# Two bank pairs in rotation, one reduce for the row maximum, a written-out order, and a rounding copy that reads SBUF

## The chip, the cores and the metric

The kernel runs on one core of a Trainium2 chip. The metric is the device time of one execution in microseconds (us): the median of three executions, before the change 281.76 us. Five engines work side by side, each through its own queue in the order in which the instructions were written: TensorE (PE, with its weight loads shown apart as PEld), VectorE (DVE), ScalarE (ACT), GpSimd (POOL), and SyncE (SP), which issues transfers. They wait for each other through semaphores.

## What is computed

A sliding-window attention with sink tokens, and behind it a gated block with a short causal convolution. The shapes are 4 batches, 8 heads, 768 positions, head width 64; the block is 512 wide.

```python
def _attn_ref(q, k, v, n_sink, window):          # n_sink = 4, window = 128
    scores = scale * np.matmul(q, k.transpose(0, 1, 3, 2))
    ...
    keep = is_sink | in_window
    scores = np.where(keep, scores, -1000000000.0)
    scores = scores - np.max(scores, axis=-1, keepdims=True)
    a = np.exp(scores)
    a = a / (np.sum(a, axis=-1, keepdims=True) + 1e-09)
    return np.matmul(a, v).astype(np.float32)

def _moe_ref(x, w_val, conv_w, w_out):           # x: attention output, heads side by side
    ...
    for k in range(K):                           # K = 5 taps
        gate_pre += conv_w[k][None, None, :] * xp[:, k:k + S, :]
    gate = 1.0 / (1.0 + np.exp(-gate_pre))
    val = x @ w_val
    return (gate * val @ w_out).astype(np.float32)
```

The three parameters of the block arrive as 64-bit floats and are decoded on the chip into a rounded high part and a rest, each in single precision.

## The kernel before

The work is cut into 24 steps. A step is one batch, one third p of the positions (256 of them) and one half of the heads (four heads, as two groups g = 0 and 1). Two steps with the same batch and third make a block m of the gated part, so there are 12 blocks. A query sees its window and the four sink keys, so the scores of one step and one group are two banks of PSUM wide.

One step runs through these events, named as in the tables below:

- kq, vv: loads of keys and queries, and of values (SP; three buffers each).
- s0, s1 (`scores`, L364): the scores of one group, 16 matmuls with 64 rows and 32 columns of the array, into the one tile `ss` of two PSUM banks. Then DVE copies the window's edge over by a mask (L369) and, in four fused instructions, adds the mask, scales by -1/8 and takes the minimum, which is minus the maximum (L374). Their output `sx` lies in SBUF, so `ss` is free as soon as DVE is done.
- e0, e1 (`exps`, L382): ACT takes the exponential of `sx`, four instructions each with a sum. rec (L387, L388) is one over the sum on DVE, norm (L396 to L403) the product on POOL, once for the window and once for the sinks.
- tx, ty (`probs_t`, L413): four transposes each on PE, into two single banks `tr`. px (L435, L437, DVE) and py (L444, ACT) write them to `wt`, with the triangle masks. sk (L418) and ts transpose the sinks' part.
- vl, si (`values`, L461, and `sinks`, L468): the attention output, into the tile `xv` of two banks. There is only one `xv`, and it is free when the convolution has read it.
- xc (L478) copies `xv` to SBUF as `xt`; xh (`x_high`, L482) rounds `xv` to the short form that the fast matmuls take; xl (L492, POOL) is the rest. hd (L486) puts the last four columns of the previous third ahead of `xv`. c4 (L496, POOL) and c0, c1 (`conv`, L504, DVE, eight instructions) are the five taps, th (L509) the gate.

A block adds v0 to v3 (`val`, L523, twelve matmuls each; v0 and v1 fill one bank, v2 and v3 the other), g0, h0, l0 and g1, h1, l1 (L534 on DVE, L538 on ACT, L542 on POOL: gate times value, its rounded form, its rest), o0 to o3 (`outp`, L553, six matmuls each) and t0, t1 (`store`).

The PSUM banks: two for `ss`, two for `xv`, two for `tr` and two for `acc`, which takes v, o, sk, the decoding of the weights and the fillers in turn.

wv and wo with a letter are the weights' loads (l) and the six stages of their decoding (a to f), for four pieces each. A filler (`busy`, L225) multiplies zeros, only to keep PE at work; there are 46 in all besides the two at L218.

The order of everything is a table of numbers: each event has a time in units of steps (`WHEN`, `EARLY`, `DECODE`, L36 to L91), the events are sorted by it (L596), and each engine gets its instructions in that order. The scheduler moves nothing.

Of the kernel before, what the change touches and what calls it, by code (L numbers as in the profile page):

```python
# [8 lines left out]
F32 = mybir.dt.float32  # L9
# [26 lines left out]
WHEN = dict(kq=-1.9615, vv=-0.3611, s0=-0.1928, e0=0.4814, s1=0.3255, e1=0.5848, rec=0.6245, vl=1.4302, norm=0.667,  # L36
            tx=0.9562, ty=1.2383, sk=1.1919, ev=1.1901, yv=1.3942, ts=1.226, val=1.8427, si=1.874, xc=2.044,
            xh=2.2668, hd=2.0069, xl=2.2917, c4=2.0938, c0=2.2838, c1=2.5363, th=2.774, v0=0.4208, v1=0.4433,
            v2=0.7542, g0=0.6699, v3=0.8679, h0=0.7252, l0=1.0416, g1=0.9504, h1=1.0551, l1=1.282, o0=1.3729,
            o1=1.5265, o2=1.3969, t0=2.127, o3=2.081, t1=2.5321, cw=-67.148)  # L40

EARLY = {("kq", 0): -111.3041, ("vv", 0): -51.6322, ("s0", 0): -67.4875, ("e0", 0): -63.9472, ("s1", 0): -63.8218,
# [39 lines left out]
DECODE = {("wv", "l"): (-149.6305, -105.8601, -107.8005, -68.4578),  # L82
# [9 lines left out]
FIRST = 16  # L92

FILL = {("scores", (0, 0)): 6, ("decode_weights", ("wv", 0, 4)): 5, ("scores", (1, 0)): 7, ("scores", (2, 1)): 4,
        ("scores", (3, 0)): 10}
SKA = 6

# [708 lines left out]
```

## Time and profile before

| | us |
|---|---|
| runs | 282.0, 281.76, 279.97 |
| median | 281.76 |
| span of the profiled execution, first to last instruction | 279.6 |
| last matmul begins / last store's copy begins | 273.24 / 273.67 |

The profiled execution is close to the fastest run: its span is 0.4 us under it. Busy times add up the stretches in which an engine had an instruction under way, so two instructions that overlap count once. The end of a matmul is modelled, so of matmuls in a row the distance from start to start is what one costs. The granted clock is 1.00 when PE runs at its full rate.

### The profile page before, as it was taken

Reading aid. Unit: us, or ns where it says so; the run is one execution under the profiler, and the core shown is the slowest. Engines: PE = TensorE matmul, PEld = TensorE weight load, DVE = VectorE, ACT = ScalarE, POOL = GpSimd, SP = SyncE. Lnnn points to the kernel's source line nnn. Section 1 sums busy time; section 2 is a strip of 40 time slices with the busy share of each in tenths; the row PEclk is TensorE's granted clock in tenths of the full one; section 3 lists DMA queues with packets and bytes.
Section 4 is the critical chain, followed back from the end, with each engine's and each line's share of the span. In section 5 each row is a group of like instructions: output and inputs, shape, how many; then the busy total and the mean of one; then the engine's idle time right before and its main releaser. Section 6 shows DMA issues by size and latency. Waiting matters only on the chain.

```text
span 279.6 us, 9649 instructions
## 1 busy us (share of the span) xinstructions
PE 264.6 (95%) x3748; PEld 211.1 (75%) x3752; DVE 221.2 (79%) x827; ACT 181.0 (65%) x605; POOL 175.4 (63%) x226
## 2 busy tenths in 40 slices
PE   8897599999999999999999999999999999999991
PEld 3444358769878879789789788788788788798880
DVE  5899969997879787986977987996896898887510
ACT  3799949838757765764875784685676667564421
POOL 3378956883965874675585757648658729647330
PEclk9999989999999999999999999999999999999997
DMA  6993952028416515516417317326336241020202
GB/s 191 328 373 129 303 158 96 4 85 291 140 49 212 157 38 194 155 41 211 140 40 246 101 67 225 101 84 205 97 93 212 87 134 56 6 75 0 77 5 82
DMA packets 27396, 36.95 MB, mean 132 GB/s; under 512 B 2256, under 2 KB 23760, under 8 KB 27344
## 3 DMA queue, kind: packets, MB, share of 16 engines
q1 hardware_dynamic: 27344, 36.27, 40.4%
q8 instruction: 31, 0.51, 0.8%
q14 instruction: 21, 0.17, 0.2%
HBM read 29.97 MB, written 6.29 MB: 130 GB/s over the span
## 4 chain that ended last, share of the span: by engine, by line
PE 77%; POOL 7%; DVE 7%; ACT 5%; issue 1%; POOLq 0%; ACTq 0%
PE acc L523 23%; PE acc L553 21%; PE xv L461 11%; PE ss L364 9%; PE tr L413 5%; PE acc L225 3%; PE xv L468 3%; POOL wx L396 2%; DVE sg L504 2%; ACT w L382 2%; DVE sx L374 2%; POOL sg L496 1%; ACT xt L478 1%; POOL xl L492 1%; POOL wol L179 1%
## 5 line engine op out<-in xcount | busy, mean ns | idle before, releaser
L396 POOL TENSOR_TENSOR wx<-w,sm 128x512 f32<-128x512 f32 x48 | 49.2, 1047 | 59.9 <-DVE sm L388 53.2
L504 DVE SCALAR_TENSOR_TENSOR sg<-xv,cw,sg 128x256 f32<-128x256 f32 x192 | 78.9, 475 | 5.9 <-POOL sg L496 5.9
L382 ACT ACTIVATE w<-sx,ngm 128x132 f32<-128x132 f32 x192 | 75.1, 399 | 4.1 <-DVE ngm L374 4.1
L523 PE MATMUL acc<-xh,wvh 128*128 128x256 f32 x192 | 49.3, 291 | 0.4 <-ACT xh L482 0.4
L523 PE MATMUL acc<-xh,wvl 128*128 128x256 f32 x192 | 47.1, 279 | 0.0
L374 DVE CUSTOM_DVE_ANT_0 sx<-ss,mask 128x132 f32<-128x132 f32 x192 | 45.2, 292 | 1.6
L553 PE MATMUL acc<-woh,gh 128*128 128x512 f32 x96 | 40.0, 416 | 0.0
L364 PE MATMUL ss<-k,q 64*32 64x168 f32 x1536 | 38.5, 309 | 1.4 <-DVE ngm L374 0.8
L523 PEld LDWEIGHTS acc<-xh,wvh 128*128 128x128 f32 x192 | 36.1, 188 | 3.8 <-DVE sg L504 1.3
L553 PE MATMUL acc<-wol,gh 128*128 128x512 f32 x96 | 38.1, 397 | 0.3 <-POOL wol L179 0.3
L553 PE MATMUL acc<-woh,gl 128*128 128x512 f32 x96 | 38.1, 396 | 0.0
L382 ACT ACTIVATION_READ_ACCUMULATOR w<-sx,ngm 128x1 f32 x192 | 37.2, 194 | 0.0
L461 PEld LDWEIGHTS xv<-wt,v 64*64 64x64 f32 x1024 | 30.3, 133 | 8.1 <-issue 5.1
L523 PEld LDWEIGHTS acc<-xh,wvl 128*128 128x128 f32 x192 | 36.1, 188 | 0.0
L542 POOL TENSOR_TENSOR gl<-sg,gh 128x512 fp32r<-128x512 f32 x24 | 31.5, 1312 | 5.7 <-ACT gh L538 5.7
L461 PE MATMUL xv<-wt,v 64*64 64x192 f32 (+2 forms) x1024 | 34.5, 278 | 0.5 <-ACT wt L444 0.5
L496 POOL TENSOR_TENSOR sg<-xt,cw 128x512 f32<-128x512 f32 x24 | 25.2, 1051 | 11.4 <-ACT xt L478 11.3
L364 PEld LDWEIGHTS ss<-k,q 64*32 64x32 f32 x1536 | 22.4, 106 | 12.8 <-issue 3.6
L492 POOL TENSOR_TENSOR xl<-xt,xh 128x512 fp32r<-128x512 f32 x24 | 30.9, 1289 | 1.7 <-ACT xh L482 1.7
L523 PE MATMUL acc<-xl,wvh 128*128 128x256 f32 x192 | 30.9, 281 | 0.9 <-POOL xl L492 0.9
L413 PE MATMUL tr<-ident,wx 128*128 128x128 f32 x192 | 28.2, 274 | 0.0
L523 PEld LDWEIGHTS acc<-xl,wvh 128*128 128x128 f32 x192 | 26.0, 188 | 1.4 <-POOL xl L492 1.3
(110 smaller groups left out, 423.5 us busy)
## 6 DMA issues: line engine op xcount, KB each, us to landing
k<-in_kt_dram SPq DMA_DIRECT2D x23, 408.0 KB, 4.0
v<-in_vt_dram SPq DMA_DIRECT2D x16, 384.0 KB, 3.3
out_dram<-osb SPq DMA_DIRECT2D x24, 256.0 KB, 2.1
q<-in_qt_dram SPq DMA_DIRECT2D x23, 256.0 KB, 4.3
raw<-in_w_val_dram SPq DMA_DIRECT2D x4, 512.0 KB, 6.7
v<-in_vt_dram SPq DMA_DIRECT2D x8, 256.0 KB, 4.2
raw<-in_w_out_dram SPq DMA_DIRECT2D x4, 512.0 KB, 6.2
vs<-in_vsk_dram SPq DMA_DIRECT2D x8, 128.0 KB, 4.1
```

The lines of the kernel that those rows point to most:

```text
L364: nc.tensor.matmul(ss[e * QB:(e + 1) * QB, j, c * n + x0:c * n + x1], q[js, g, (4 * c + e) * QB:(4 * c + e + 1) * QB], k[js, g, (2 * c + e ...
L374: nc.vector.tensor_tensor_reduce(out=sx[:, j, c], in0=sv[:, j, c, :PK], in1=mask[:, c if p == 0 else 2], op0=ALU.add, op1=ALU.min, scale=- ...
L382: nc.scalar.activation(out=w[:, g, j, c], in_=sx[:, j, c], func=AF.Exp, scale=-1.0, bias=ngm[:, g, j, c:c + 1], accum_out=sm[:, g, j, c:c ...
L396: nc.gpsimd.tensor_tensor(out=t[:, n].rearrange("p c h x -> p h c x"), in0=w[:, :, :, at], in1=sm.to_broadcast([P, 4, 2, D]), op=ALU.mult)
L413: nc.tensor.transpose(out=x[:, o:o + P], identity=ident, in_=ws[s][:, n, c, 2 * g:2 * g + 2].rearrange("p j x -> p (j x)"))
L461: nc.tensor.matmul(acc[o * D:(o + 1) * D, g, x0 + h * D:x0 + (h + a1 - a0 + 1) * D], v[js, g, n], t[js, g, n, a0:a1 + 1].rearrange("p a r ...
L492: nc.gpsimd.tensor_tensor(out=xl[:, g], in0=xts[s], in1=xh[:, g].bitcast(F32), op=ALU.subtract)
L496: nc.gpsimd.tensor_tensor(out=sg[s // 2][:, g], in0=xts[s], op=ALU.mult, in1=cw[:, g, KT - 1:].to_broadcast([P, 2, PQ]))
L504: nc.vector.scalar_tensor_tensor(out=g, in0=x, scalar=a, in1=g, op0=ALU.mult, op1=ALU.add)
L523: nc.tensor.matmul(acc[:, h], a[:, kc, cs], x[:, kc], start=(n == 0), stop=(n == 11))
L542: nc.gpsimd.tensor_tensor(out=gl, in0=g, in1=gh.bitcast(F32), op=ALU.subtract)
L553: nc.tensor.matmul(acc, a[:, kc, ts], x[:, kc], start=(kc + n == 0), stop=(kc + n == 5))
```

## The change

Eight banks are given out anew. Two pairs of banks rotate: each scores half, and each step's transposes (now tx alone, eight in a row), take the next pair. `xv` keeps its two banks. The two single banks are now called homes: a user takes the first from a list and puts it back where its reader is issued. For the first two blocks the values are copied out of their bank by ACT (`val_copy`, y0 and y1), so that the gate's product reads SBUF.

For the second and third p the maximum is one `tensor_reduce` over the two banks and a small product with -1/8, and the exponentials read the pair in PSUM. The first p keeps the four fused instructions. The mask has two planes instead of three.

The rounding copy xh reads `xt` in SBUF instead of `xv` in PSUM.

The tables of numbers are gone. The order is a list of names. The identity, the two sign matrices, the blanks and the warm-up of the exponential are events of that list too, the index patterns of the masks are issued in one go, and three of the first loads (q of step 0 in two parts, wv piece 0) are issued from ACT's queue. Fillers: 38, and six at the start. The keys of steps 6 and 10 are loaded ahead of those of step 5, into the same three buffers.

```diff
-WHEN = dict(kq=-1.9615, vv=-0.3611, s0=-0.1928, e0=0.4814, s1=0.3255, e1=0.5848, rec=0.6245, vl=1.4302, norm=0.667,
...
+ORDER = """
+fill.7 load_conv wvl.0 fill.10 masks kq.0 conv_weights wvl.2 wva.0 wvb.0 wvc.0 wvd.0 s0.0 s1.0 e0.0 blanks
+fill.5 signs wva.2 wvb.2 e1.0 rec.0 wve.0 wvl.1 wva.1 wvb.1 fill.4 kq.1 s1.1 wvc.2 wvf.0 wvd.2 kq.2 wol.1 s0.1
...
+COPIES = 2
...
-    ps_t = ctx.enter_context(tc.tile_pool(name="ps_t", bufs=2, space=PSUM))
-    ps_a = ctx.enter_context(tc.tile_pool(name="ps_a", bufs=2, space=PSUM))
...
+    pairs = [ps_s.tile([P, 2, 512], F32, name=f"pr{n}") for n in range(2)]
...
+    def pair():
+        pairs.append(pairs.pop(0))
+        return pairs[-1]
...
+    homes = [ps_a.tile([P, 512], F32, name=f"ac{n}") for n in range(2)]
...
     def busy(n):
-        t = ps_a.tile([P, 512], F32, name="acc", tag="acc")
+        t = homes.pop(0)
...
+        homes.append(t)
...
+            (nc.scalar if s == 0 else nc.sync).dma_start(out=q[:, hs], in_=qt[b, gs, :, p * PQ:(p + 1) * PQ].rearrange("g p x -> p g x"))
...
+        ss = pair()
...
+        if p:
+            sxs[s, g] = sv
+            nc.vector.tensor_reduce(out=ngm[:, g], in_=sv[:, :, :, :PK], axis=mybir.AxisListType.X, op=ALU.max)
+            nc.vector.tensor_scalar(out=ngm[:, g], in0=ngm[:, g], scalar1=-0.125, scalar2=None, op0=ALU.mult)
+            return
...
-                nc.scalar.activation(out=w[:, g, j, c], in_=sx[:, j, c], func=AF.Exp, scale=-1.0,
+                nc.scalar.activation(out=w[:, g, j, c], in_=sx[:, j, c, :PK], func=AF.Exp,
+                                     scale=0.125 if steps[s][1] else -1.0,
...
-    def probs_t(s, n):
-        trs[s, n] = x = ps_t.tile([P, 512], F32, name="tr", tag="tr")
...
+    def probs_t(s):
+        trs[s] = x = pair()
+        for n in range(2):
...
     def x_high(s):
-        g, o = slice(2 * steps[s][2], 2 * steps[s][2] + 2), KT - 1
-        nc.scalar.activation(out=xs[s // 2][0][:, g], in_=accs[s][:, :, o:o + PQ], func=AF.Copy)
+        nc.scalar.activation(out=half(xhs, s, "xh", F32R), in_=xts[s], func=AF.Copy)
...
+    def val_copy(m, u):
+        t = p2.tile([P, 4, P, 2], I32, name="vc", tag="raw", bufs=4)
+        x = t.rearrange("p k m t -> p (k m t)")[:, :2 * PQ].bitcast(F32)
+        nc.scalar.activation(out=x, in_=vacc[m, u], func=AF.Copy)
+        homes.append(vacc[m, u])
+        vacc[m, u] = x
...
-        for _, f, args in sorted(events, key=lambda e: e[0]):
+        for n in ORDER.split():
+            f, args = events[n]
             f(*args)
-            if (f.__name__, args) in FILL:
-                busy(FILL[f.__name__, args])
```

What the new order does is seen at two places. The first is ACT's queue while the first block is being prepared. Here `wt` (L444, new L462) is py of step 1, `skt` is ts of step 1, `xt` and `xh` of L478 and L482 (new L494 and L502) are the copies of the attention output, `w,sm` the exponentials and `wo_p`, `wvl`, `woh` stages of the decoding. Before:

```order
L444 ACTIVATE wt<-tr 128x2x3x64
L193 ACTIVATE wvl<-acc 128x4x128
L163 ACTIVATE woh<-wo_t 128x512
L426 ACTIVATE skt<-acc,blk 128x128 x2
L147 ACTIVATE wo_p<-raw 128x512
L478 ACTIVATE xt<-xv 128x512
L382 ACTIVATE w,sm<-sx,ngm 128x132 x4
L482 ACTIVATE xh<-xv 128x512
```

Now, from the same copy `wt` of step 1 on:

```order
L462 ACTIVATE wt<-pr_86 128x2x3x64
L132 ACTIVATE wo_p<-raw 128x512
L438 ACTIVATE skt<-ac_93,blk 128x128 x2
L502 ACTIVATE xh<-xt 128x512
L152 ACTIVATE wo_p<-raw 128x512
L494 ACTIVATE xt<-xv 128x512
L502 ACTIVATE xh<-xt 128x512
L392 ACTIVATE w,sm<-pr_87,ngm 128x132 x4
```

The four exponentials that stood between the plain copy of step 1 and its rounding copy now stand behind it, and the rounding copy of step 0 (ahead of the rows shown in the first list) has moved to just before them. On PE, before, the first scores half of step 3 (s0.3) and ten fillers stood ahead of the values of step 1 (vl.1); now six fillers stand ahead of tx.1, six behind the last decoding sum of wv, and sk.1 and one scores half (s1.3) between these and vl.1.

The second place is PE's queue in the middle of the run. Before, the second scores half of step 11 (L364) stands alone between the transposes of step 10 (L413) and the first val product of block 4 (v0, L523), and such a place comes in most blocks:

```order
L553 MATMUL acc<-woh,gl 128x512
L418 MATMUL acc<-ident,skb_108 128x128
L413 MATMUL tr<-ident,wx 128x128 x4
L364 MATMUL ss<-k,q 32x168 x16
L523 MATMUL acc<-xh,wvh 128x256
```

Now two scores halves (s1.12 and s0.13), each in a pair of its own (`pr_87`, `pr_86`), and the values of step 10 (vl.10, L480) with their sinks (L487) follow each other, between output products (L582):

```order
L582 MATMUL ac_93<-woh,gl 128x512
L369 MATMUL pr_87<-k,q 32x168 x16
L369 MATMUL pr_86<-k,q 32x168 x16
L480 MATMUL xv<-wt,v 64x192 x8
L480 MATMUL xv<-wt,v 64x128 x4
L480 MATMUL xv<-wt,v 64x64 x4
L487 MATMUL xv<-skt,vh 128x256 x2
L582 MATMUL ac_92<-woh,gh 128x512
```

Scores halves have moved together: what used half of the array's rows stood in 43 separate stretches from the first v0 on, and stands in 31.

More of the change, by code (lines that the diff above doesn't have):

```diff
@@ L186, in total @@
         one, plus, minus = unit
-        acc.append(a := bank())
+        acc.append(a := bank.pop(0))
         nc.tensor.matmul(a, one, tf, start=True, stop=False)
@@ L194, in low, with banded @@
                              else acc[0], func=AF.Copy)
+        bank.append(acc.pop())
     return (bias, bits, share, high) + ((add,) if unit is None else (rest, scaled) if cut else (total, low))
-def banded(ctx, tc, wts, cw, zero, ident, scalars, flag, qt, kt, vt, vsk, w_val, conv_w, w_out, out):
+def banded(ctx, tc, wts, cw, zero, ident, warm_up, scalars, flag, qt, kt, vt, vsk, w_val, conv_w, w_out, out):
     nc = tc.nc
@@ L266, in banded @@
     prev = cn.tile([P, D], F32, name="prev")
-    mask = cn.tile([P, 3, PK], F32, name="mask")
+    mask = cn.tile([P, 2, PK], F32, name="mask")
     none = cn.tile([P, 2, KT - 1], F32, name="none")
@@ L306, in banded, with signs, blanks @@
     minus = cn.tile([P, P], F32R, name="minus")
-    nc.gpsimd.tensor_scalar(out=plus, in0=ident, scalar1=1.0, scalar2=None, op0=ALU.mult)
-    nc.gpsimd.tensor_scalar(out=minus, in0=ident, scalar1=-1.0, scalar2=None, op0=ALU.mult)
+    def signs():
+        make_identity(nc, ident)
+        nc.gpsimd.tensor_scalar(out=plus, in0=ident, scalar1=1.0, scalar2=None, op0=ALU.mult)
+        nc.gpsimd.tensor_scalar(out=minus, in0=ident, scalar1=-1.0, scalar2=None, op0=ALU.mult)
     skb = [cn.tile([P, P], F32, name=f"skb{n}") for n in range(2)]
+    def blanks():
+        for t in skb:
+            nc.gpsimd.memset(t, 0.0)
     raws, dec = {}, {}
@@ L328, in decode_weights @@
             dec[n, c] = _decode(nc, p2, raws[n, c], n, *hl, [P, 4, P] if n == "wv" else [P, DM],
-                                (ident, plus, minus), None if (n, c) in CUT else lambda: ps_a.tile([P, 512], F32, name="acc", tag="acc"))
+                                (ident, plus, minus), None if (n, c) in CUT else homes)
         dec[n, c][stage]()
@@ L451, in values @@
         v, t, x0 = vv[s], probs[s], KT - 1
-        accs[s] = acc = ps_v.tile([P, 2, 512], F32, name="xv", tag="xv")
+        bank = ps_v.tile([P, 2, 512], F32, name="xv", tag="xv")
+        accs[s] = acc = bank[:, :, :KT - 1 + PQ]
         tiles = [(g, j, j if g == 0 else 1 - j) for g in range(2) for j in range(2)]
@@ L547, in outp @@
         if h == 0:
-            vacc[m, 2 + i] = ps_a.tile([P, 512], F32, name="acc", tag="acc")
+            vacc[m, 2 + i] = homes.pop(0)
         acc = vacc[m, 2 + i]
@@ L557, in store @@
         nc.scalar.activation(out=ob, in_=vacc[m, 2 + i], func=AF.Copy, scale=0.5)
+        homes.append(vacc[m, 2 + i])
         at = (2 * (m % NP) + i) * P
         nc.sync.dma_start(out=out[m // NP, at:at + P, :], in_=ob)
[L562 to L576 removed]
@@ L592, in banded @@
-    busy(FIRST - 2)
-    for t in skb:
-        nc.gpsimd.memset(t, 0.0)
+    acts = {"kq": (load_kq, ()), "vv": (load_v, ()), "s0": (scores, (0,)), "s1": (scores, (1,)), "e0": (exps, (0,)),
+            "e1": (exps, (1,)), "rec": (recip, ()), "norm": (normalise, ()), "tx": (probs_t, ()), "px":
+            (probs_x, ()), "py": (probs_y, ()), "sk": (sinks_t, ()), "ts": (sinks_e, ()), "vl": (values,
+            ()), "si": (sinks, ()), "xc": (x_copy, ()), "xh": (x_high, ()), "hd": (x_head, ()), "xl":
+            (x_low, ()), "c4": (conv_last, ()), "c0": (conv, ((0, 1),)), "c1": (conv, ((2, 3),)), "th":
+            (gate, ()), "sv": (sink_values, ()), "v0": (val, (0, 0)), "v1": (val, (0, 1)), "v2": (val,
+            (1, 0)), "v3": (val, (1, 1)), "g0": (gated, (0,)), "h0": (gated_h, (0,)), "l0": (gated_l,
+            (0,)), "g1": (gated, (1,)), "h1": (gated_h, (1,)), "l1": (gated_l, (1,)), "y0": (val_copy,
+            (0,)), "y1": (val_copy, (1,)), "o0": (outp, (0, 0)), "o1": (outp, (0, 1)), "o2": (outp, (1,
+            0)), "o3": (outp, (1, 1)), "t0": (store, (0,)), "t1": (store, (1,))}
@@ new lines, in banded @@
+    events = {f"{n}.{x}": (f, (x,) + args) for n, (f, args) in acts.items() for x in range(len(steps))}
+    for f in (masks, signs, blanks, warm_up, scalars, flag, load_conv, conv_weights):
+        events[f.__name__] = f, ()
+    for n in ("wv", "wo"):
+        for c in range(4):
+            events[f"{n}l.{c}"] = load_weights, (n, c)
+            for k in range(6):
+                events[f"{n}{'abcdef'[k]}.{c}"] = decode_weights, (n, c, k)
+    for n in range(1, 20):
+        events[f"fill.{n}"] = busy, (n,)
@@ L736 @@
     with ExitStack() as c:
-        banded(c, tc, wts, cw, zero, ident, scalars, flag, qt, kt, vt, vsk,
+        banded(c, tc, wts, cw, zero, ident, warm_up, scalars, flag, qt, kt, vt, vsk,
                w_val, conv_w, w_out, out)
```

175 lines of the change are left out of this document (95 added, 80 removed), and 48 rows, old and new, of tables (DECODE, EARLY).

## The prediction

> **What bounds the kernel now.** I read the page's first and fourth part first, then the waits of PE, then windows of the span, then the timelines of the engines at the places found.
>
> ```profile
> PE 264.6 (95%) x3748; PEld 211.1 (75%) x3752; DVE 221.2 (79%) x827; ACT 181.0 (65%) x605; POOL 175.4 (63%) x226
> ...
> PE 77%; POOL 7%; DVE 7%; ACT 5%; issue 1%; POOLq 0%; ACTq 0%
> ```
>
> PE is busy in 95% of the span, and 77% of the chain that ended last lies on it. So a term counts if it shortens what PE does or waits for. The waits of PE, in us in total, times, longest:
>
> ```profile
> PE acc L225 <- ACT wvl L193: 2.1, 1, 2.1
> ...
> PE acc L523 <- POOL xl L492: 0.9, 2, 0.5
> ```
>
> The longest wait stands in the startup and is a filler's. Windows of the span (length, then busy time of PE, weight loads, DVE, ACT, POOL; granted clock) divide it:
>
> ```profile
> 7.30:43.20 35.90, 29.31 (x407) 16.47 (x410) 31.67 (x119) 29.89 (x102) 25.08 (x31) 0.95 0.77 258
> 43.18:98.00 54.82, 54.20 (x798) 45.00 (x799) 47.46 (x172) 38.98 (x131) 39.12 (x46) 1.00 0.39 126
> 98.00:273.70 175.70, 175.02 (x2531) 147.51 (x2529) 137.67 (x516) 109.47 (x371) 108.65 (x136) 1.00 0.34 107
> ```
>
> From 43.18 to 273.70 PE idles only 54.82 - 54.20 + 175.70 - 175.02 = 1.3 us. There is nearly no waiting left to take away in that stretch, only the cost of PE's own instructions. Ahead of it PE is busy in 29.31 of 35.90 us, and part of that are fillers, so there the other engines set the pace. The startup and PE's own spacing are therefore the two places from which a gain can come.
>
> **The startup.** These are PE's rows, then ACT's, POOL's and again PE's around the first block; the bracket is the idle time before a row and what ended it.
>
> ```profile
> 33.51 0.48 PE L225 MATMUL acc<-zero 128*128 128x512 bf16 x1 [2.05 <-ACT wvl L193]
> 34.21 3.31 PE L225 MATMUL acc<-zero 128*128 128x512 bf16 x8 [0.22 <-DMA q<-in_qt_dram]
> 37.45 1.21 PE L461 MATMUL xv<-wt,v 64*64 64x192 f32 x32
> 38.59 0.51 PE L468 MATMUL xv<-skt,vh 128*128 128x256 f32 x2
> ...
> 39.13 0.60 ACT L478 ACTIVATE xt<-xv 128x512 f32<-128x512 f32 x1 [4.09 <-PE xv L468]
> ...
> 41.19 0.57 ACT L482 ACTIVATE xh<-xv 128x512 fp32r<-128x512 f32 x1
> ...
> 41.84 1.29 POOL L492 TENSOR_TENSOR xl<-xt,xh 128x512 fp32r<-128x512 f32 x1 [0.98 <-ACT xh L482]
> ...
> 43.18 0.50 PE L523 MATMUL acc<-xl,wvh 128*128 128x256 f32 x2 [0.39 <-POOL xl L492]
> ```
>
> PE waits 2.05 us for the last low part of wv, and then runs ten fillers before the values of step 1 (37.45), at half the clock:
>
> ```profile
> 34.00:35.00 1.00, 0.79 (x2) 0.30 (x2) 0.98 (x3) 1.00 (x3) 1.00 (x2) 0.50 1.01 403
> ```
>
> Eight of them take 3.31 us, 0.41 each. For the sinks of step 1 ACT idles 4.09 us, and when it has the plain copy, two groups of four exponentials stand around the rounding copy: it ends at 41.19 + 0.57 = 41.76. The rest xl follows and PE's product continues at 43.18. After that PE never waits long again.
>
> Now the ten fillers are gone from that place (six stand ahead of tx.1, six after the last decoding sum), and xh.1 stands directly behind xc.1. I take the ACT engine as what sets the end, since PE's own events ahead of v0 are the same with eight fillers fewer. Ahead of 41.76, ACT had 29.89 - (43.20 - 41.76) = 28.45 us of work from 7.30 on and 41.76 - 7.30 - 28.45 = 6.0 of idling. The new order keeps the same exponentials (seven groups) and copies ahead of xh.1, without one rounding copy of w_out and the decoding of the taps, 1.2 in all by copies of some 0.6. The idling of 4.09 goes, provided that si.1 is done by about 36. The start is later: 23 matmuls of zeros ahead of s0.0 instead of 16, and seven at 0.29 (row below) to 0.37 (5.13 over 14) are 2.0 to 2.6 later, of which ACT's decoding of wv fills a part; I count 0 to 2.0 for ACT.
>
> ```profile
> 2.21 5.13 PE acc L225 x14
> ...
> 8.01 1.47 PE L225 MATMUL acc<-zero 128*128 128x512 bf16 x5
> ```
>
> So xh.1 ends at 41.76 - 4.09 - 1.2 + (0 to 2.0) = 36.5 to 38.5, and 37.5 is the middle. The gain there is 4.3; I take off 0.5, since POOL has xl of step 0 and a rest of w_out ahead of xl.1. The term is **-3.8**. Its ends: -2.0, if POOL, DVE or PE bind where ACT no longer does (two thirds of the idling kept, as 4.09 x 2/3 = 2.7 would leave 1.6 to 2.0), and -4.6, if only ACT binds and it starts nearly as early.
>
> **Excursions into half the array.** Scores and values use 64 rows (64*32, 64*64 in the rows), the rest of PE's work uses 128. Starts on PE in a steady stretch:
>
> ```profile
> 92.09 0.40 PE L468 MATMUL xv<-skt,vh 128*128 128x256 f32 x2
> 92.33 0.60 PE L413 MATMUL tr<-ident,wx 128*128 128x128 f32 x4
> ...
> 97.96 0.40 PE L553 MATMUL acc<-wol,gh 128*128 128x512 f32 x1
> 98.20 0.40 PE L553 MATMUL acc<-woh,gl 128*128 128x512 f32 x1
> 98.53 0.80 PE L364 MATMUL ss<-k,q 64*32 64x168 f32 x32
> 99.26 1.21 PE L461 MATMUL xv<-wt,v 64*64 64x192 f32 x32
> 100.40 0.51 PE L468 MATMUL xv<-skt,vh 128*128 128x256 f32 x2
> 100.74 0.60 PE L413 MATMUL tr<-ident,wx 128*128 128x128 f32 x4
> ```
>
> An output product costs 0.24 from start to start (97.96 to 98.20), but 0.33 where scores follow: 0.1 for going in. From scores to values (both 64 rows) it is 0.73, the scores' usual price, so no toll lies between them. The sinks' pair takes 0.24 where it stands among 128-row work (92.09 to 92.33), and 0.34 behind values (100.40 to 100.74): 0.1 for coming out. From the first v0 on there were 43 such stretches and are 31 now, because two score halves stand together, or a half and the values. 12 x 0.2 = 2.4, so **-2.4**. The ends are 0, if the weight loads ahead of the joined halves cost the same time, and -2.4.
>
> **The tail.** Before, xl of the last step came late by one wait:
>
> ```profile
> 262.47 0.39 PE L523 MATMUL acc<-xl,wvh 128*128 128x256 f32 x2
> 263.34 0.51 PE L523 MATMUL acc<-xl,wvh 128*128 128x256 f32 x2 [0.48 <-POOL xl L492]
> ```
>
> Now eighteen output products (o2, o1, o3 of block 10, 18 x 0.24 = 4.3) stand between si.23 and the last v0 instead of six (1.4). The wait goes: **-0.5**. What stands behind the last product (its gate, output and store) is the same.
>
> **The maximum, and the pairs.** Four fused instructions took from 217.26 to 218.12, since they overlap, though their group has 292 ns each:
>
> ```profile
> 217.26 0.29 DVE L374 CUSTOM_DVE_ANT_0 sx<-ss,mask 128x132 f32<-128x132 f32 x1
> ...
> 218.12 1.65 DVE L504 SCALAR_TENSOR_TENSOR sg<-xv,cw,sg 128x256 f32<-128x256 f32 x4
> ```
>
> A reduce of a PSUM tile is not in the trace. The nearest rows read PSUM on DVE with 512 and 256 elements, and the small product is like L387:
>
> ```profile
> L435 DVE TENSOR_TENSOR wt<-tr,cur 128x512 f32<-128x512 f32 x24 | 16.5, 687 | 9.2 <-PE tr L413 9.2
> L369 DVE COPY_PREDICATED ss<-low,ss 128x256 f32<-128x256 uint8 x48 | 20.4, 425 | 6.9 <-PE ss L364 6.6
> L387 DVE TENSOR_SCALAR sm<-sm 128x8 f32<-128x8 f32 x24 | 4.6, 192 | 1.1 <-ACT w L382 1.1
> L382 ACT ACTIVATE w<-sx,ngm 128x132 f32<-128x132 f32 x192 | 75.1, 399 | 4.1 <-DVE ngm L374 4.1
> ```
>
> (687 - 425) / 256 = 1.02 ns per element, so 528 elements take 0.70, with 0.19 for the product: 0.9 against 0.86. DVE gains nothing; below, 0.4 could be won if the reduce took as little as L369, above, 0.7 more lost if it took twice the 0.70. Over 32 halves it is about +0.1 each, 3 us on an engine that is busy 137.67 of 175.70: covered. One page speaks against this edit: the Trainium skill, "VectorE: DVE Perf Modes", section "Rules for kernel authors", says of tensor_reduce on a hot path to expect no fast mode and calls it the slowest operation of DVE. From that page's 2293 ns for 2048 elements without a fast mode, 0.59 is an estimate for 528; with it the tight places below would be 0.1 shorter each and the time some 0.8 lower, 275.8. No row here shows a reduce.
>
> What changes is who holds the bank. Before, `ss` was free when DVE was done; now the exponentials of 32 halves read the pair, so from the end of the scores it takes 0.45 (L369), 0.9 and 4 x 0.40 of ACT (L382), with some 0.3 between engines: 3.2 us. Against that, two pairs rotate. Counting PE's work between a half and the next user of its pair by the order of the list and the starts above, 24 of the 32 halves have 4.2 us or more, and eight have 3.7 to 4.2 (after s1.15, s0.5, s1.9, s1.14 the least). The cover is 0.5 to 1.0 us there, and is gone when ACT has another group of exponentials (1.6) or DVE a convolution (1.65, row 218.12) ahead. I take an average wait of 0.12 for the eight, **+1.0**; the ends are 0 and +4, 0.5 each. The one tile `xv` is used again after 5.3 us of PE's work at the least, against about 5.1 needed; that is in the same term.
>
> **The keys of step 5** are loaded behind those of steps 6 and 10, into the buffer that s1.4 frees on PE.
>
> ```profile
> k<-in_kt_dram SPq DMA_DIRECT2D x23, 408.0 KB, 4.0
> ...
> 72.30 0.87 PE tr L413 x8
> ```
>
> Between s1.4 and s0.5 PE has 4.1 us of work (twelve output products 2.9, sinks 0.34, eight transposes 0.87); the landing takes 4.0 and the issue some 0.4: **+0.5**, ends 0 and +1.2. Queued behind that issue on SP are loads with 5.7 us and more to spare.
>
> **The rounding copy** reads SBUF. The same shape exists from both places:
>
> ```profile
> L482 ACT ACTIVATE xh<-xv 128x512 fp32r<-128x512 f32 x24 | 14.3, 595 | 0.1
> L538 ACT ACTIVATE gh<-sg 128x512 fp32r<-128x512 f32 x24 | 15.1, 628 | 13.9 <-DVE sg L534 13.9
> ```
>
> 33 ns x 24 = 0.8 us of ACT, plus a wait of some 0.1 for the copy just before it. ACT is busy 65% and xl has room behind it, so 0. It lies on the path only at xh.1 (0.13, within the first term), and takes one reader off `xv`, which the convolution still holds. The four val copies (0.6 each) and the events moved to other places in the startup (masks, identity, signs, taps, three issues on ACT's queue) are 0: ACT's cover is its 35% of idle time, in the startup it is inside the 0 to 2.0.
>
> **The sum.** -3.8 - 2.4 - 0.5 + 1.0 + 0.5 = -5.2. The profiled execution has a span of 279.6, and would have 274.4. It stands 0.4 under the fastest of the runs and 2.2 under their median; with the median the forecast is 281.76 - 5.2 = **276.6**.
>
> **The rivals.** *The clock halves again.* The new startup has waits of PE too, by my chain none over 1.4 us. After 2.05 us the clock was 0.50; if 1.4 is enough, ten matmuls of 512 columns take 0.41 instead of 0.24, 1.7 more: 278.3. Against it speaks the shorter gap. The Trainium skill, "TensorE: Matmul & The Clock Gate", section "What's actually happening", puts the fall to half rate behind an idle window of about 3.4 us; by that rule this rival has no chance at all and 276.6 stands. The trace does not agree: 2.05 us of waiting were enough.
>
> *Excursions cost what they did.* Then 2.4 is missing: -2.8, 279.0. For it speaks that weight loads are 75% busy, and joined halves may wait for theirs; against it the 0.73 from scores to values.
>
> *The pairs wait at the eight tight places.* With +4 instead of +1 the gain is 2.2: 279.6.
>
> *Slower: the exponentials hold the pairs everywhere.* If ACT or DVE runs later than PE's order allows, every one of the 32 halves makes its pair's next user wait. Without the term for the pairs the gain is 6.2, so it decides from 6.2 / 32 = 0.19 each, and is slower by over 1% from (6.2 + 2.8) / 32 = 0.28. At 0.35 it is 11.2: 286.8. For it speaks that the path after the scores grew from 1.3 to 3.2 us; against it that 24 halves have at least 1.0 us over that.
>
> **How the numbers follow.** Forecast 0.50; clock 0.12; excursions 0.10; tight pairs 0.18; slower 0.10. One per cent, 2.8 us, is about what a measurement of this kernel can tell from no change. Faster by more: 0.50 + 0.12 + half of 0.10 = 0.67. Within: the other half and 0.18 = 0.23. Slower: 0.10. The low end: -4.6 - 2.4 - 0.5 = -7.5, with 1 us for the spread of the runs, 273.3. The sum of all bad ends is -2.0 + 0 + 0 + 4 + 1.2 = +3.2; two of them seldom meet, so I stop at 282.0, which holds the first three rivals and leaves out the fourth.
>
> **What would show it.** Right, if PE's third part of the first val product runs near 39.4 instead of 43.18, and ACT has no idle time over 2 us ahead of it; if the granted clock stays 1.00 from 20 to 45; if the stretch from the first xl product to the last matmul (43.18 to 273.7, 230.5 us) shrinks by about 1.4, with 2.4 less in the spacing around scores and 1.5 more in waits of PE for exponentials and k; if the reduce takes 0.6 to 0.8. Wrong, if scores or transposes wait for ACT's exponentials at many places, if scores wait for k, or if the startup ends after 41.

## The result, and the profile after

| | before | after |
|---|---|---|
| median, 9 runs each, us | 281.39 | 284.44 |
| lowest to highest, us | 279.41 to 282.0 | 282.3 to 286.13 |
| span of the profiled execution, us | 279.6 | 284.2 |

The ratio after to before is 1.0133, with a 95% interval from 1.0099 to 1.0166. The change made the kernel slower by 1.3%, or 3.0 us, where 5.2 us less was forecast. A run takes 1.7 to 2.0 us more than its span (285.94 for the profiled execution of 284.2). So the profiled execution of before, with its span of 279.6, is a run near the median and not one near the fastest, as was said ahead of the result; that of after lies 1.5 us over its own median.

The page of the changed kernel, first and fourth part:

```profile
PE 261.3 (92%) x3748; PEld 215.0 (76%) x3748; DVE 232.2 (82%) x635; ACT 179.8 (63%) x609; POOL 174.9 (62%) x226
...
PE 66%; DVE 21%; issue 4%; ACT 4%; DMA 2%; POOL 2%; SPq 0%; DVEq 0%; ACTq 0%
```

PE is busy for 3.3 us less and the chain is 66% PE's instead of 77%. DVE's share of the chain has gone from 7% to 21%, though DVE runs 192 instructions fewer: more of what PE waits for now goes back to DVE, directly or through ACT and POOL. The waits of PE in the changed kernel (us in total, times, longest):

```profile
PE xv L480 <- ACT wt L462: 2.1, 1, 2.1
PE xv L480 <- DVE sg L523: 2.0, 3, 1.0
PE pr L369 <- ACT w L392: 1.6, 2, 1.4
PE ac L582 <- POOL gl L571: 1.5, 1, 1.5
...
PE xv L480 <- issue: 1.0, 1, 1.0
PE ac L430 <- ACT osb L586: 0.8, 1, 0.8
PE ac L582 <- POOL wol L164: 0.8, 1, 0.8
```

Laid against the sum of the forecast, with the third part of the first val product as the end of the startup:

| | forecast | before to after | us |
|---|---|---|---|
| startup ends | -3.8 | 43.18 to 42.65 | -0.5 |
| PE's listed waits behind it | -0.5 + 1.0 + 0.5 | 1.1 to 7.6 | +6.5 |
| the rest of PE's time up to the last matmul | -2.4 | 229.0 to 227.0 | -2.0 |
| last matmul to the end of the span | 0 | 6.36 to 6.98 | +0.6 |
| span | -5.2 | 279.6 to 284.2 | +4.6 |

So in this execution PE's spacing shrank, the startup hardly got shorter, and new waits took more than all of it. Groups of DVE show where they start, the reduce and the small product above all (line, engine, operation, shapes, count; busy, mean ns; idle before):

```profile
L378 DVE TENSOR_REDUCE ngm<-pr 128x4 f32<-128x528 f32 x32 | 22.6, 707 | 1.1
...
L379 DVE TENSOR_SCALAR ngm<-ngm 128x4 f32<-128x4 f32 x32 | 14.8, 463 | 1.1
...
L399 DVE RECIPROCAL sm<-sm 128x8 f32<-128x8 f32 x24 | 4.9, 203 | 0.8
```

The reduce is what the rows had given, 707 ns. The product over four numbers is not: 463 ns on the mean, from 170 to 1132. The shortest is the work; what is over it adds up to 9.4 us over the 32. Not every small instruction in SBUF does this: the third row, the reciprocal of eight numbers, took 202 to 206 ns all 24 times, also the eight times that it began while POOL was at work. DVE's and POOL's timelines beside each other, at four of the long ones (the third is a product of the sums):

```profile
90.68 1.07 DVE L379 TENSOR_SCALAR ngm<-ngm 128x4 f32<-128x4 f32 x1
...
92.86 0.82 DVE L379 TENSOR_SCALAR ngm<-ngm 128x4 f32<-128x4 f32 x1
...
98.17 1.27 DVE L398 TENSOR_SCALAR sm<-sm 128x8 f32<-128x8 f32 x1
...
100.78 1.02 DVE L379 TENSOR_SCALAR ngm<-ngm 128x4 f32<-128x4 f32 x1
```

```profile
90.68 1.04 POOL L515 TENSOR_TENSOR sg<-xt,cw 128x512 f32<-128x512 f32 x1
...
92.61 2.04 POOL L407 TENSOR_TENSOR wx<-w,sm 128x512 f32<-128x512 f32 x2
...
98.15 1.27 POOL L571 TENSOR_TENSOR gl<-sg,gh 128x512 fp32r<-128x512 f32 x1 [2.57 <-ACT gh L567]
...
100.48 1.29 POOL L571 TENSOR_TENSOR gl<-sg,gh 128x512 fp32r<-128x512 f32 x1
```

Each long product on DVE begins while a product on POOL is under way, and ends with it: 91.75 and 91.72, 99.44 and 99.42, 101.80 and 101.77. The one at 92.86 ends at 93.68, with the first of the two of wx (93.66). Thirteen of the 32 took longer than 0.32 us; each of these ends within 0.1 us of the end of a product on POOL, and they hold 9.1 of the 9.4 us. No view of waits names it: it stands in the profile as busy time of a short instruction. The Trainium skill, "SBUF — State Buffer", section "Who interferes with whom", has the rule: DVE and GpSimd share a pair of SBUF ports as an exclusive lock, and a tensor_scalar that can use a two-port mode, or a DVE instruction with two SBUF inputs against a GpSimd instruction that reads SBUF, blocks until the holder's whole instruction is done. The trace agrees to 0.05 us at all four places.

What follows from it in the startup, on DVE, POOL and ACT:

```profile
33.99 3.22 DVE L523 SCALAR_TENSOR_TENSOR sg<-xv,cw,sg 128x256 f32<-128x256 f32 x8
37.12 1.47 DVE L137 TENSOR_SCALAR wo_t<-wo_p 128x512 int32<-128x512 int32 x1
...
37.04 1.27 POOL L510 TENSOR_TENSOR xl<-xt,xh 128x512 fp32r<-128x512 f32 x1 [0.23 <-ACT xh L502]
...
39.40 0.70 ACT L152 ACTIVATE wo_p<-raw 128x512 f32<-128x512 uint32 x1 [2.44 <-DVE wo_t L139]
40.01 0.58 ACT L494 ACTIVATE xt<-xv 128x512 f32<-128x512 f32 x1
40.62 0.63 ACT L502 ACTIVATE xh<-xt 128x512 fp32r<-128x512 f32 x1
```

A decoding product that takes 0.42 alone runs beside xl of step 0, which ends at 38.31, and takes 1.47. ACT waits 2.44 us for the decoding, and only behind that come the plain and the rounding copy of step 1. PE had the sinks of step 1 done at about 39.

### The profile page after: what moved, and what is told of

It reads as the page before. It is cut to its first block, busy times and chain, and to the rows that moved or that the text cites. A ratio compares the mean times of both kernels' runs of the same rounds, so it can differ in the third digit from the quotient of the medians.

```text
span 284.2 us, 9480 instructions
## 1 busy us (share of the span) xinstructions
PE 261.3 (92%) x3748; PEld 215.0 (76%) x3748; DVE 232.2 (82%) x635; ACT 179.8 (63%) x609; POOL 174.9 (62%) x226
## 4 chain that ended last, share of the span: by engine, by line
PE 66%; DVE 21%; issue 4%; ACT 4%; DMA 2%; POOL 2%; SPq 0%; DVEq 0%; ACTq 0%
PE ac L582 18%; PE ac L542 17%; PE xv L480 10%; PE pr L369 8%; DVE sg L523 5%; PE pr L425 5%; PE xv L487 3%; DVE ngm L378 2%; ACT w L392 2%; PE ac L219 2%; DMA q<-in_qt_dram 2%; DVE pr L374 2%; DVE wo_t L137 1%; DVE sm L398 1%; DVE sg L561 1%
## 5 line engine op out<-in xcount | busy, mean ns | idle before, releaser
L523 DVE SCALAR_TENSOR_TENSOR sg<-xv,cw,sg 128x256 f32<-128x256 f32 x192 | 77.5, 476 | 8.4 <-ACT xv L506 5.3
L392 ACT ACTIVATE w<-pr,ngm 128x132 f32<-128x132 f32 x128 | 45.4, 369 | 13.8 <-DVE ngm L379 11.6
L542 PE MATMUL ac<-xh,wvh 128*128 128x256 f32 x192 | 49.5, 290 | 1.0 <-ACT xh L502 0.7
L542 PE MATMUL ac<-xh,wvl 128*128 128x256 f32 x192 | 48.1, 283 | 0.0
L480 PEld LDWEIGHTS xv<-wt,v 64*64 64x64 f32 x1024 | 31.5, 136 | 13.5 <-issue 3.9
L480 PE MATMUL xv<-wt,v 64*64 64x192 f32 (+2 forms) x1024 | 35.5, 283 | 6.2 <-ACT wt L462 2.1
L582 PE MATMUL ac<-woh,gl 128*128 128x512 f32 x96 | 38.0, 395 | 1.6 <-POOL gl L571 1.5
L369 PE MATMUL pr<-k,q 64*32 64x168 f32 x1536 | 35.8, 311 | 3.5 <-ACT w L392 1.6
L582 PE MATMUL ac<-woh,gh 128*128 128x512 f32 x96 | 38.7, 403 | 0.1
L582 PE MATMUL ac<-wol,gh 128*128 128x512 f32 x96 | 37.8, 394 | 0.8 <-POOL wol L164 0.8
L542 PEld LDWEIGHTS ac<-xh,wvh 128*128 128x128 f32 x192 | 36.6, 191 | 2.6 <-ACT xh L502 0.9
L542 PEld LDWEIGHTS ac<-xh,wvl 128*128 128x128 f32 x192 | 36.7, 191 | 0.2
L392 ACT ACTIVATE w<-sx,ngm 128x132 f32<-128x132 f32 x64 | 25.0, 394 | 5.9 <-DVE ngm L384 5.9
```

The source lines that it names most:

```text
L369: nc.tensor.matmul(ss[e * QB:(e + 1) * QB, j, c * n + x0:c * n + x1], q[js, g, (4 * c + e) * QB:(4 * c + e + 1) * QB], k[js, g, (2 * c + e ...
L392: nc.scalar.activation(out=w[:, g, j, c], in_=sx[:, j, c, :PK], func=AF.Exp, scale=0.125 if steps[s][1] else -1.0, bias=ngm[:, g, j, c:c + ...
L480: nc.tensor.matmul(acc[o * D:(o + 1) * D, g, x0 + h * D:x0 + (h + a1 - a0 + 1) * D], v[js, g, n], t[js, g, n, a0:a1 + 1].rearrange("p a r ...
L523: nc.vector.scalar_tensor_tensor(out=g, in0=x, scalar=a, in1=g, op0=ALU.mult, op1=ALU.add)
L542: nc.tensor.matmul(acc[:, h], a[:, kc, cs], x[:, kc], start=(n == 0), stop=(n == 11))
L582: nc.tensor.matmul(acc, a[:, kc, ts], x[:, kc], start=(kc + n == 0), stop=(kc + n == 5))
```

## The experiments

Twelve kernels, against before on the same chip. Before measured 280.25 in the first four, 281.38 in the next four and 281.15 in the last.

| kernel | median, us | ratio to before, 95% interval |
|---|---|---|
| after, maxima in PSUM | 280.49 | 0.999 [0.9958, 1.0022] |
| after, product with two SBUF inputs | 284.37 | 1.012 [1.0055, 1.0185] |
| after, four fused instructions | 281.8 | 1.0051 [1.0022, 1.0079] |
| after, rounding copy from PSUM | 296.9 | 1.0567 [1.0503, 1.0632] |
| after, maxima in PSUM and no addition | 278.94 | 0.9942 [0.9904, 0.9979] |
| the same with four buffers of keys | 277.84 | 0.9911 [0.9882, 0.994] |
| before, rounding copy from SBUF | 280.17 | 0.9995 [0.9958, 1.0031] |
| before, product in SBUF behind the maximum | 287.37 | 1.0234 [1.0159, 1.0308] |
| before, the same through PSUM | 293.52 | 1.0467 [1.0404, 1.0531] |
| before, unused product in SBUF | 286.58 | 1.0213 [1.0147, 1.0278] |
| before, unused product from PSUM | 282.35 | 1.0051 [1.0014, 1.0088] |
| before, no addition | 279.47 | 0.9974 [0.9941, 1.0006] |

### The product reads PSUM, or has two SBUF inputs

```diff
-nc.vector.tensor_reduce(out=ngm[:, g], in_=sv[:, :, :, :PK], axis=mybir.AxisListType.X, op=ALU.max)
-nc.vector.tensor_scalar(out=ngm[:, g], in0=ngm[:, g], scalar1=-0.125, scalar2=None, op0=ALU.mult)
+m = ss[:, :, 2 * n:2 * n + 2]
+nc.vector.tensor_reduce(out=m, in_=sv[:, :, :, :PK], axis=mybir.AxisListType.X, op=ALU.max)
+nc.vector.tensor_scalar(out=ngm[:, g], in0=m, scalar1=-0.125, scalar2=None, op0=ALU.mult)
```

> One edit to the changed kernel: the reduce writes its four maxima into spare columns of the scores' own PSUM pair, and the small product reads them there; everything else as changed. Theory A (the small products on DVE wait until a product under way on POOL has ended, when both their operands lie in SBUF; 9.4 us of DVE in the changed kernel's 32 products): every small product takes 0.2 us or less, the waits of PE behind block one fall from 7.6 to 3 or 4, and the time falls by 3 to 6 us, to 278.5 to 281.5. Theory B (the pairs are held too long, whatever the product takes, or the order is bad): the small products get shorter but the time stays within 1.5 us of 284.4. Theory C (the rounding copy from SBUF is to blame): as B.

The second kernel keeps the reduce and changes the product alone:

```diff
-nc.vector.tensor_scalar(out=ngm[:, g], in0=ngm[:, g], scalar1=-0.125, scalar2=None, op0=ALU.mult)
+nc.vector.scalar_tensor_tensor(out=ngm[:, g], in0=ngm[:, g], scalar=-0.125, op0=ALU.mult, op1=ALU.add,
+                               in1=zero.bitcast(F32)[:, :4].rearrange("p (j c) -> p j c", c=2))
```

> One edit to the changed kernel: the small product is a scalar_tensor_tensor with a tile of zeros added, so it has two operands in SBUF and cannot use a fast mode; all else as changed. If any DVE instruction with two operands in SBUF waits for a product on POOL too, its durations stay spread from 0.2 to 1.1 us and the time stays at 284. If only the single-operand form waits, it takes 0.2 us throughout and the time is that of the kernel with the maxima in PSUM.

The groups of the product, with the maxima in PSUM:

```profile
L380 DVE TENSOR_SCALAR ngm<-pr 128x4 f32<-128x4 f32 x32 | 5.2, 161 | 1.1
```

and with two inputs in SBUF:

```profile
L379 DVE SCALAR_TENSOR_TENSOR ngm<-ngm,zero 128x4 f32<-128x4 f32 x32 | 13.6, 424 | 1.1
```

From PSUM the product takes 161 ns each time, and the time falls from 1.0133 of before to 0.999, about 4 us: theory A, with 280.49 inside its 278.5 to 281.5. With two inputs in SBUF it keeps waiting (424 ns), and so does the time, 284.37. So it is not the one form alone that waits: two inputs in SBUF are enough, as the same section of the Trainium skill's "SBUF — State Buffer" has it. The startup is not where the two kernels differ, its end is at 40.84 and 40.61. Behind it PE's listed waits are 4.9 us against 7.9, and the rest of PE's time is 225.5 against 227.0. The 4.9 are more than the 3 to 4 expected.

### The maximum as before, and the rounding copy as before

```diff
-        if p:
-            sxs[s, g] = sv
...
-            return
-        sxs[s, g] = sx = p2.tile([P, 2, 2, PK], F32, name="sx", tag="sx")
+        sxs[s, g] = sx = p2.tile([P, 2, 2, PK], F32, name="sx", tag="sx", bufs=4)
...
-                    out=sx[:, j, c], in0=sv[:, j, c, :PK], in1=mask[:, c], op0=ALU.add,
+                    out=sx[:, j, c], in0=sv[:, j, c, :PK], in1=mask[:, 2 if p else c], op0=ALU.add,
```

> One part of the change undone: all steps take the maximum with the four fused instructions, as before, whose output lies in SBUF (four buffers instead of two); the pair is free when DVE is done. Bank pairs, order and the copy from SBUF stay. Theory A and B both expect a gain, since it takes away the product and the long hold of the pair: 277 to 280. If A alone is the cause, it is no better than the kernel with the maxima in PSUM by more than 1 us; if the hold of the pair matters (B), it is better by 2 us or more. If the new order itself loses, it stays above 282.

281.8 is above the 277 to 280 expected, and 1.3 us more than with the maxima in PSUM. Holding the pair through the exponentials costs nothing that shows; the rival by which the pairs are the trouble falls. Its profile has one wait of 3.54 us in the startup, from which the difference may come, so the 1.3 are not put down to the maximum.

```diff
-        nc.scalar.activation(out=half(xhs, s, "xh", F32R), in_=xts[s], func=AF.Copy)
+        nc.scalar.activation(out=half(xhs, s, "xh", F32R), in_=accs[s][:, :, KT - 1:], func=AF.Copy)
```

> One part of the change undone: the rounding copy reads the attention's output in PSUM again; all else as changed. Theory A and B: within 1 us of 284.4. Theory C: below 282.5.

No theory expected this: 296.9. In this order the part of the change that reads SBUF is worth some 12 us (1.0567 against 1.0133 of before). The waits of PE in this kernel:

```profile
PE pr L369 <- ACT w L392: 4.6, 4, 1.8
PE xv L480 <- ACT xh L502: 4.0, 4, 1.5
PE ac L542 <- ACT xh L502: 2.6, 1, 2.6
```

The list puts many rounding copies late on ACT. If they read PSUM, the one tile `xv` is held until then: the values wait for xh (4.0), and what follows them is late everywhere; the listed waits behind the startup add up to 18.2 us instead of 7.6, and from 113.8 on the granted clock is 0.50 for 3.4 us, which no other profile here has in the middle of the run. To see whether the edit has a worth of its own, it was made alone in the old order:

```diff
-        nc.scalar.activation(out=xs[s // 2][0][:, g], in_=accs[s][:, :, o:o + PQ], func=AF.Copy)
+        nc.scalar.activation(out=xs[s // 2][0][:, g], in_=xts[s], func=AF.Copy)
```

> The kernel before with the rounding copy alone changed: it reads the plain copy in SBUF. If the edit is worth what its undoing cost in the new order (12 us), the old order gains too; if its worth comes from where the new order puts the rounding copies (late, while the next values wait for the tile), it is 280 to 281.5 here, no change.

0.9995 of before: nothing. Its worth is that of the place at which the copy stands.

### The cost of the wait, in the kernel before

```diff
+        if p:
+            nc.vector.tensor_scalar(out=ngm[:, g], in0=ngm[:, g], scalar1=1.0, scalar2=None, op0=ALU.mult)
```

> The kernel before with one small DVE product added in place in SBUF (times 1.0) behind the four fused instructions of every half of the second and third p: 32 of them. Theory A: they wait for POOL's products, 5 to 11 us of waits in all on DVE, as in the changed kernel, and the time rises by 1 us or more over the twin that reads PSUM. Rival (such waits come from the new order's timing only): 0.2 us each, and the time is that of the twin.

The twin lets the fused instructions write their minima to PSUM:

```diff
-accum_out=ngm[:, g, j, c:c + 1])
+accum_out=(ss[:, j, 2 * n + c:2 * n + c + 1] if p else ngm[:, g, j, c:c + 1]))
+        if p:
+            nc.vector.tensor_scalar(out=ngm[:, g], in0=ss[:, :, 2 * n:2 * n + 2], scalar1=1.0, scalar2=None, op0=ALU.mult)
```

> The twin of the kernel before with the product added: the four minima go into spare columns of the scores' PSUM tile and the product by 1.0 reads them there, writing to SBUF. Both theories: 0.2 us each, 32 x 0.2 = 6 us more on DVE in all, and the time within 1.5 us of before (280 to 282).

The first shows the waits in the old order (416 ns on the mean, 7.9 us over the shortest) and 287.37. The twin was to be the cheap one and is the dearest, 293.52, so the pair tells nothing of the wait. DVE's timeline of the twin shows why:

```profile
109.87 0.29 DVE L374 CUSTOM_DVE_ANT_0 sx<-ss,mask 128x132 f32<-128x132 f32 x1
110.09 0.14 DVE L374 DVE_READ_ACCUMULATOR2_ANT ss<- 128x1 f32 x1
110.27 0.29 DVE L374 CUSTOM_DVE_ANT_0 sx<-ss,mask 128x132 f32<-128x132 f32 x1
```

With the minimum going to PSUM, the fused instructions follow each other every 0.40 us instead of 0.22, and the product at their end keeps the one tile `ss` longer. So a second pair of twins adds products that nothing waits for by its data, between the masked copy and the fused instructions:

```diff
+        if p:
+            nc.vector.tensor_scalar(out=jk, in0=jk, scalar1=1.0, scalar2=None, op0=ALU.mult)
```

> The kernel before with 32 small DVE products of four numbers that nothing waits for by its data: in place on a small tile in SBUF, between the masked copy and the four fused instructions of each half of the second and third p. Theory A: they wait for POOL's products, 5 to 11 us in all, and since the fused instructions and all behind them on DVE stand in the queue, the time is 2 to 5 us above that of its twin that reads PSUM. Rival: 0.2 us each and the time of the twin.

and the same with `in0=ss[:, :, 500:502]`, columns that no score uses:

> The twin: the same 32 products at the same place, but they read spare columns of the scores' tile in PSUM. Both theories: 0.16 to 0.2 us each without waits, about 5 us more on DVE, and the time 0 to 3 us over before.

The group in SBUF:

```profile
L375 DVE TENSOR_SCALAR jk<-jk 128x4 f32<-128x4 f32 x32 | 19.2, 599 | 0.0
```

and from PSUM:

```profile
L375 DVE TENSOR_SCALAR jk<-ss 128x4 f32<-128x4 f32 x32 | 5.2, 162 | 1.1
```

Same count, same place, same four numbers: 599 against 162 ns, 286.58 against 282.35 us. Of the 32 in SBUF, 22 took longer than 0.31 us, and all 22 end within 0.1 us of the end of a product on POOL. The waits alone are 14 us of DVE and cost 4.2 us of time, where DVE is busy 79% of the span without them. They were more than the 5 to 11 expected; the price in time is as expected.

### A version that beats both

```diff
-        nc.vector.tensor_scalar(out=sm, in0=sm, scalar1=1e-9, scalar2=None, op0=ALU.add)
         nc.vector.reciprocal(out=sm, in_=sm)
```

> The changed kernel with the maxima in PSUM, and the product that adds 1e-9 to the sums of the exponentials left out (each sum holds the exponential of its own maximum, so it is about 1 or more, and the addition changes nothing in single precision). Theory A (waits of DVE's SBUF products for POOL): 4 us fewer of such waits on DVE than the kernel with the maxima in PSUM, and 24 instructions fewer; of PE's waits only those behind it go, so 278.5 to 280. Theory B (DVE's waits are off the path by now): 280 to 281.

> The kernel before without the addition of 1e-9 to the sums, and nothing else: does the old order gain from it too? Its 24 products waited only 0.8 us in all, so theory A expects 279.5 to 281.5, no change to speak of.

> The changed kernel with the maxima in PSUM and without the addition of 1e-9, and with four buffers for keys and queries instead of three. The forecast counted 0.5 us (0 to 1.2) for loads that come late because of the three buffers; the kernel with three had one wait of 1.1 us for a q. If that wait is the whole of it, 0.5 to 1.5 us less: 277.5 to 278.5; if it is covered elsewhere, 278.9.

The edit of the last is `bufs=4` for the tiles k and q. All three kernels leave out the 1e-9 that the reference adds to the sums. Without the addition, the kernel with the maxima in PSUM comes to 0.9942 (278.94, inside theory A's 278.5 to 280), and with four buffers to 0.9911 of before; the old order without the addition is at 0.9974, whose interval holds no change. So once DVE's products are out of POOL's way, the new order is faster than before as it stands. That it is faster than the old order without the addition is not shown: 0.9942 and 0.9974 have intervals that overlap, and while the interval of 0.9911 lies just below, the old order was not measured with four buffers. The two last steps in the new order overlap in their intervals too, and the profile does not show the fourth buffer doing what it was meant for: with three, a scores half waited 1.13 us for q, and with four still

```profile
172.30 0.81 PE L369 MATMUL pr<-k,q 64*32 64x168 f32 x32 [1.03 <-DMA q<-in_qt_dram]
```

What the fourth buffer is worth stays open. So do the waits for gl and wol in the first two blocks, 2.3 to 3.2 us together in these kernels and in after; an order that moves them was not tried. The trace of after suggests where the one for gl comes from. Ahead of gl in the first block (48.65 to 53.41), two small products on POOL take 1.11 and 0.69 us where 0.24 and 0.29 are usual, and gl takes 1.66 instead of 1.29. DVE has instructions with two inputs in SBUF under way beside them: decoding, and the gate's product, which reads the values that were copied to SBUF. That looks like the same clash with POOL as the one that waits, and its 1.6 us are about the 1.47 that PE waits; no run tests it.

## Why the prediction was wrong, point by point

**The maximum.** This is the step that failed. It put "0.19 for the product", "+0.1 each, 3 us on an engine that is busy 137.67 of 175.70: covered", from the mean of L387. The reduce was right (0.70 forecast, 0.707 measured; the 0.59 estimated from the Trainium skill's page "VectorE: DVE Perf Modes" was too low). The product took 0.463, with up to 0.96 of waiting, and DVE's products by a constant, these, those of the sums and the decoding's together, stood 17.3 us over the shortest of their rows where before it was 2.6. The extra time was not covered: undoing the waits of the 32 gave back 4 us, of the 8.2 that lie between the forecast of -5.2 and the medians' +3.0. The rows of before held the warning: of the 24 products of L387 most took 0.16, one 0.835. POOL is busy 63% of the span with products of 1.05 to 1.3 us, so a DVE product that comes at any time waits 0.63 x 0.55 = 0.35 us on the mean: an estimate from rows of the page, 11 us for 32, against 9.4 measured here and 7.9 and 14.1 in the two kernels of before with a product in SBUF.

**The pairs.** The forecast feared waits for the exponentials (+1.0, up to +4, and the slower rival 11.2). In the steady part PE waited 0.26 us for them, and in the startup once 1.36. The kernel was slower by another mechanism than that of the slower rival, and the early release of the pairs, by the fused instructions, gained nothing that shows.

**The startup.** "I take the ACT engine as what sets the end" was wrong: ACT waits 2.44 us for decoding on DVE, behind a convolution of 3.2 us and a wait for POOL. The bound of -2.0, "if POOL, DVE or PE bind", was passed as well: -0.5. That size belongs to this execution. In the profiles of the six other kernels with the new order the third part came between 40.25 and 42.44, that is -2.9 to -0.7, and the waiting products do not decide it: with the maxima in PSUM it came at 40.84, and with two inputs in SBUF, where the products wait as they do in after, at 40.61, with only 0.27 us of waiting by ACT for the decoding. In after, PE ran at half the clock for 6.9 us of the startup instead of the 3.4 of the others, and DVE waited 1.01 us for transposes just ahead of the convolution named above. The -3.8 itself was reached in none.

**The clock.** The forecast saw no wait over 1.4 us ahead; there was one of 2.11, and the clock halved within it, at 24.75. The values of step 0 wait for ACT's copy, and ACT waits 1.36 us for DVE, where two decoding instructions that usually take 0.42 and 0.69 take 1.31 and 1.42 beside products on POOL:

```profile
25.32 2.19 PE L480 MATMUL xv<-wt,v 64*64 64x192 f32 x32 [2.11 <-ACT wt L462]
...
26.00:28.00 2.00, 2.00 (x37) 1.49 (x37) 1.93 (x4) 0.74 (x3) 1.66 (x2) 0.50 0.68 236
```

**The excursions** came out near the forecast, -2.4 against -2.0, but in part by luck. The -2.0 are all of PE's time outside its listed waits, and with the maxima in PSUM the same remainder is -3.4. The scores alone, from start to start, went from 29.2 to 28.0 us, since two joined halves cost less than twice one (121.05 to 122.36 below, 1.31 for two, against 2 x 0.73), which the forecast did not count. All else that PE does, where the 0.1 for going in and the 0.1 for coming out would show, went from 199.7 to 199.0 only. The joined halves:

```profile
121.05 1.37 PE L369 MATMUL pr<-k,q 64*32 64x168 f32 x64
122.36 1.55 PE L480 MATMUL xv<-wt,v 64*64 64x64 f32 x48
```

**The tail and the keys.** The wait for xl at the end went. The keys of step 5 did not make PE wait, but the q of a later step did, 0.71: the term has its size and another place. It had counted on 4.0 us to land for k; now k took 4.7 and q 5.2, on the median, after 4.0 and 4.3 before.

**The rounding copy** was put at 0. That holds for the old order. In the new one it is what makes the order possible, some 12 us.

**What the product does not explain.** With the maxima in PSUM the profiled span is 278.0, 1.6 us under that of before, where 5.2 were forecast. Of the 3.6 between, the startup has about 1.5 (-2.3 instead of -3.8), PE's listed waits 2.8 (4.9 instead of 1.1, so +3.8 against +1.0) and the tail 0.4, while the remainder of PE's time saved 1.0 more than forecast. The largest of those waits, for gl and wol with 2.3, had no term in the sum. Their cause was not tested.

## What to carry to other kernels

Price a small product by a constant on DVE from SBUF to SBUF, or a DVE instruction with two inputs in SBUF, not by its usual duration but by that plus POOL's busy share times half of POOL's usual instruction, and look at the maximum of its row, not the mean; the wait stands as busy time and in no list of waits. The reciprocal in SBUF did not wait here. If the product's source can lie in PSUM instead, 32 of them cost 0.16 us each and no more, but look at what the instruction that writes the source then costs: the reduce took about the same, the fused instructions did not. And when a stage is full, work out which engine sets its end by following all of them to the last copy, since a term that rests on one engine's row of work ends where another engine feeds it.

## What the hardware showed unexpectedly

A wait of PE of 1.11 us can be followed by a stretch at half the clock. In the kernel with the maxima in PSUM it ends at 18.27, no earlier wait since the first matmuls is longer, and the clock falls at 18.85; the windows of 2 us show it:

```profile
18.27 0.90 PE L369 MATMUL pr<-k,q 64*32 64x168 f32 x32 [1.11 <-DVE ngm L385]
...
18.00:20.00 2.00, 1.73 (x33) 0.97 (x34) 1.93 (x14) 2.00 (x13) 2.00 (x3) 0.71 1.03 296
20.00:22.00 2.00, 2.00 (x5) 1.07 (x4) 1.73 (x6) 2.00 (x11) 1.67 (x5) 0.50 1.02 360
22.00:24.00 2.00, 1.82 (x41) 1.31 (x39) 2.00 (x3) 1.83 (x7) 2.00 (x2) 0.93 1.07 371
```

But the length of that wait does not settle it. The changed kernel has the same one, and its clock stays at 1.00 until 24.75:

```profile
17.84 0.81 PE L369 MATMUL pr<-k,q 64*32 64x168 f32 x32 [1.11 <-DVE ngm L384]
```

Of the seven profiles of the new order, all with this wait, three show the fall within 1.0 us of its end and four do not. The old order has the clearest pair. Ahead of its ten fillers PE waits 2.04 us in the kernel with the unused product from PSUM, and 2.03 in the one without the addition. In the first the clock falls and the values begin 3.94 us after the fillers' start, in the second it stays at 1.00 and they begin after 2.25. What decides is open. Each of these stretches in the startup lasts 3.4 us, or twice that in after.

The Trainium skill, "TensorE: Matmul & The Clock Gate", section "What's actually happening", asks for an idle window of about 3.4 us; the trace does not agree, neither here nor after the 2.11 us above. The first rival, with 1.4 us as its condition, was better than the 0.12 it was given: every profile of the new order has such a stretch in its startup, though before has one too. The runs of before themselves fall into two groups, in the second set of runs 279.4 to 279.9 at a mean clock of 0.992 to 0.995 and 281.2 to 282.6 at 0.986 to 0.989. The pair above fits one such stretch as their difference: 282.62 at 0.986 with it, 279.55 at 0.994 without.

The other surprise is that the fused instruction with a running minimum loses its overlap when the minimum goes to PSUM: 0.40 instead of 0.22 us from one to the next.
